# Decode attention with a gated FFN: one load for the first cache group, ring slots on 512-byte addresses, and two projections with the activations stationary

## The chip, the cores and the metric

The kernel runs on one core of one Trainium2 chip. The metric is device time in microseconds (us); less is better. Eight runs of the kernel before gave a median of 127.25 us, from 126.56 to 128.67.

## The reference, cut to what matters

Eight sequences decode one token each. The width D is 512; attention has 32 query heads and 8 key/value heads of 128, and looks at the last 1024 positions of a cache of 4096. All inputs are bf16.

```
xn = layernorm(x)                                   # x: 8 x 512
q  = xn @ wq                                        # wq: 512 x 4096
scores = einsum(q, k) * 128**-0.5                   # 4 query heads per key/value head
o  = softmax(scores) @ v                            # k, v: 8 x 8 x 1024 x 128 of the cache's window
s  = o.reshape(8, 4096) @ wo                        # wo: 4096 x 512
g  = silu((gelu(xn @ w_gate) * (xn @ w_up)) @ w_down)   # F = 1792
return x + s * g
```

The windows of k and v are 16 MiB each, wq and wo 4 MiB each, and the three FFN matrices 1.75 MiB each: 47.45 MB that are each read once.

## The kernel before, in words

The order of every engine's instructions is the order of the code (`manual_schedule`); there is no planner. All large loads are issued from SP into a ring of 22 SBUF slots of 8 KB per partition (`slot`, 1 MB each): first the keys of group 0, then the four row blocks of wq, then keys and values of the 16 groups in turn, then w_gate, w_up and w_down in two halves each, then wo in four blocks. A group is one key/value head and four sequences (I = 4): a slot holds its 4 x 1024 keys, 32 per partition. SP's loads use eight completion semaphores in rotation, which the four small loads of `xq_sb` on ACT's queue use as well. A load waits until the load that had its semaphore before has landed, so about eight are under way at once. From the 23rd slot on, a load waits also until PE has let go of the slot's old content.

Group 0 of the keys is loaded in four DMAs of 32 rows (L88, every fourth partition); all other groups in one DMA of 128 rows (L90).

PE works in blocks of eight key columns. `transpose_block` (L261) transposes eight 128x128 pieces of keys into PSUM, and DVE copies them to `kT` (L270). `score_block` (L272) multiplies them with the queries, and after four blocks ACT takes the exponentials (L288). `value_block` (L308) runs six blocks later: it sums the exponentials by a matmul with ones (L300) and multiplies them with the values (L313). Two key blocks are transposed before `project_q` (L242), which every score needs. `expand_out` and `select_out` (L333, L350) bring the attention output of eight heads into the layout in which wo is read.

`project_q` makes q already transposed: each 128x128 piece of wq is the stationary operand, and the eight columns of `xnT_sb` are streamed; 128 matmuls, then one DVE cast (L254). `ffn_up` (L377) does the same with w_gate and w_up: 2 x 14 x 4 = 112 matmuls, for which every seventh column of a half of F is picked as stationary. The chain of elementwise steps for gelu (L393 to L406) works on 128 x 112 values. `ffn_down` (L408) and `project_out` (L364) have the activations stationary (8 columns) and stream the weights, in four column groups: output quarter q goes to PSUM partitions 32q to 32q+7.

At the end the program calls `expand_out(3)`, `ffn_up`, `select_out(3)`, `ffn_down`, `project_out(0)` to `(3)`, then the product `tmp` (L457), the sum with the residual `xq_sb`, which is bf16 (L459), and four stores of 2 KB.

PSUM: `ps_m` has two buffers of one bank; q, the sums, the outputs, the FFN results and the transposes of the tail all take them in turn.

SBUF: the pools `consts` and `persist` lie in front of the ring. In the built program the first slot starts at byte 25056 of a partition, which is 97 x 256 + 224; slots are 8192 bytes apart, so that all start 224 bytes past a multiple of 256.

Of the kernel before, what the change touches and what calls it, by code (L numbers as in the profile page):

```python
# [7 lines left out]
ACT = mybir.ActivationFunctionType  # L8
ALU = mybir.AluOpType
AX = mybir.AxisListType  # L10
BF16 = mybir.dt.bfloat16
FP32 = mybir.dt.float32
# [3 lines left out]
def kernel(  # L16
# [13 lines left out]
    nc = tc.nc  # L30

    B, Sq, D = A_x.shape
    Hkv, Sk, Dh = A_k_cache.shape[1], A_k_cache.shape[2], A_k_cache.shape[3]
    Hq = A_wq.shape[1] // Dh
    rep = Hq // Hkv
    W = min(4096, max(256, Sk // 4))
    win0 = Sk - W
    F = B_w_gate.shape[1]
    P = nc.NUM_PARTITIONS
    NDC = D // P  # L40
# [4 lines left out]
    I = 4  # L45
    R = P // I
    C = W // R
# [4 lines left out]
    NB = C // CB  # L52
    SLOT = C * Dh

    JF = F // 2 // P
    NQ = D // P

    consts = ctx.enter_context(tc.tile_pool(name="consts", bufs=1))
    persist = ctx.enter_context(tc.tile_pool(name="persist", bufs=1))
    ring = ctx.enter_context(tc.tile_pool(name="ring", bufs=22))  # L60
    kT_pool = ctx.enter_context(tc.tile_pool(name="kT_pool", bufs=4))
    p_pool = ctx.enter_context(tc.tile_pool(name="p_pool", bufs=3))
    small = ctx.enter_context(tc.tile_pool(name="small", bufs=3))
# [2 lines left out]
    ps_m = ctx.enter_context(tc.tile_pool(name="ps_m", bufs=2, space=bass.MemoryType.PSUM))  # L66
# [9 lines left out]
    def slot():  # L76
        return ring.tile([P, SLOT], BF16, name="slot")

    k_t, v_t, wo_t = {}, {}, {}
    wq_t, wg_t, wu_t, wd_t = [], [], [], []  # L80

    def load_cache(src, g, split=False):
        t = slot()
        hkv, b0 = g // GPH, (g % GPH) * I
        rows = src[b0 : b0 + I, hkv, win0:Sk, :].rearrange("i (r c) d -> i r (c d)", c=C)
        if split:
            for i in range(I):
                nc.sync.dma_start(out=t[i::I, :], in_=rows[i])  # L88
        else:
            nc.sync.dma_start(out=t, in_=rows.rearrange("i r m -> r i m"))  # L90
        return t

    def load_k(g, split=False):
        k_t[g] = load_cache(A_k_cache, g, split)

    def load_v(g):
        v_t[g] = load_cache(A_v_cache, g)
# [7 lines left out]
    def load_ffn():  # L105
        for dst, src in ((wg_t, B_w_gate), (wu_t, B_w_up)):
            for a in range(2):
                t = slot()
                nc.sync.dma_start(
                    out=t[:, 0 : 2 * F],  # L110
                    in_=src[a * 2 * P : (a + 1) * 2 * P, :].rearrange(
                        "(p k) f -> p (k f)", k=2
                    ),
                )
                dst.append(t[:, 0 : 2 * F].rearrange("p (k f) -> p k f", k=2))
        for a in range(2):
            t = slot()
            nc.sync.dma_start(
                out=t[:, 0 : JF * D],
                in_=B_w_down[a * JF * P : (a + 1) * JF * P, :].rearrange(  # L120
                    "(p j) d -> p (j d)", j=JF
                ),
            )
            wd_t.append(t[:, 0 : JF * D].rearrange("p (j d) -> p j d", j=JF))


    HS = SLOT // D
# [8 lines left out]
                nc.sync.dma_start(out=t[:, lo:hi, :], in_=src[:, lo:hi, :])  # L136
        wo_t[m] = t

    load_k(0, split=True)
    load_wq()  # L140
    for g in range(1, NG):
        load_k(g)
# [3 lines left out]
    for m in range(NM):  # L146
# [3 lines left out]
    ident = consts.tile([P, P], BF16, name="ident")  # L150
    nc.vector.memset(ident, 0.0)
    nc.gpsimd.affine_select(  # L152
        out=ident, in_=ident, compare_op=ALU.not_equal, fill=1.0, base=0,
# [10 lines left out]
        out=sel, in_=sel, compare_op=ALU.not_equal, fill=1.0, base=0,  # L164
# [4 lines left out]
        out=diag, in_=sel.rearrange("p r i -> p i r"), axis=AX.X, op=ALU.add  # L169
    )  # L170
    nc.vector.tensor_scalar(
        out=diag, in0=diag, scalar1=1.0, scalar2=30000.0, op0=ALU.subtract, op1=ALU.mult
# [6 lines left out]
        out=hmask, in_=hmask, compare_op=ALU.is_ge, fill=0.0, base=0,  # L179
# [3 lines left out]
        out=hmask, in_=hmask, compare_op=ALU.is_ge, fill=0.0, base=B - 1,  # L183
# [5 lines left out]
        out=bsel3, in_=bsel3, compare_op=ALU.not_equal, fill=1.0, base=0,  # L189
# [4 lines left out]
        out=bsel_f, in_=bsel3.rearrange("p h b -> p b h"), axis=AX.X, op=ALU.add  # L194
# [5 lines left out]
    xq_sb = persist.tile([P, P], BF16, name="xq_sb")  # L200
# [17 lines left out]
        op0=ALU.subtract, op1=ALU.mult,  # L218
    )

    xnT_sb = persist.tile([P, NDC, B], BF16, name="xnT_sb")
    xpT_sb = persist.tile([P, NDC, B], BF16, name="xpT_sb")
    qT_all = persist.tile([P, Hkv, B, rep], BF16, name="qT_all")
    oT_all = persist.tile([P, Hq, B], BF16, name="oT_all")
    hT_sb = persist.tile([P, 2 * JF, B], BF16, name="hT_sb")
    g_sb = persist.tile([P, P], FP32, name="g_sb")

    s_ps = ps_s.tile([P, P], FP32, name="s_ps")
# [2 lines left out]
    def transpose_x():  # L231
        t = ps_m.tile([P, 2, NDC, B], BF16, name="m_ps")
        for k in range(NDC):
            nc.tensor.transpose(t[:, 0, k, :], xhat[:, k * P : (k + 1) * P], ident[0:B, 0:B])  # L234
        xp = xhat.rearrange("b (a p k) -> b a k p", a=2, k=2)
        for a in range(2):
            for k in range(2):
                nc.tensor.transpose(t[:, 1, 2 * a + k, :], xp[:, a, k, :], ident[0:B, 0:B])
        nc.vector.tensor_copy(out=xnT_sb, in_=t[:, 0])
        nc.vector.tensor_copy(out=xpT_sb, in_=t[:, 1])  # L240

    def project_q():  # L242
        q_ps = ps_m.tile([P, Hq, B], FP32, name="m_ps")
        for k in range(NDC):
            for h in range(Hq):
                nc.tensor.matmul(  # L246
                    q_ps[:, h, :],
                    wq_t[k][:, h * Dh : (h + 1) * Dh],
                    xnT_sb[:, k, :],
                    start=(k == 0 and h == 0),  # L250
                    stop=(k == NDC - 1),
                    skip_group_check=True,
                )
        nc.vector.tensor_copy(  # L254
            out=qT_all, in_=q_ps.rearrange("p (h j) b -> p h b j", j=rep)
        )


    kT, sc, pT, oT = {}, {}, {}, {}
# [114 lines left out]
                )  # L374


    def ffn_up():  # L377
        gu_ps = ps_m.tile([P, 2, 2 * JF, B], FP32, name="m_ps")
        for w, wt in enumerate((wg_t, wu_t)):
            for j in range(2 * JF):  # L380
                f0 = (j // JF) * (F // 2) + j % JF
                for k in range(NDC):
                    nc.tensor.matmul(  # L383
                        gu_ps[:, w, j, :],
                        wt[k // 2][:, k % 2, f0 : f0 + (P - 1) * JF + 1 : JF],
                        xpT_sb[:, k, :],
                        start=(k == 0),
                        stop=(k == NDC - 1),
                    )
        shape = [P, 2 * JF, B]  # L390
        zT, uT = gu_ps[:, 0], gu_ps[:, 1]
        z2 = persist.tile(shape, FP32, name="z2")
        nc.scalar.activation(out=z2, in_=zT, func=ACT.Square)  # L393
        nc.vector.tensor_scalar(  # L394
            out=z2, in0=z2, scalar1=0.044715, scalar2=1.0, op0=ALU.mult, op1=ALU.add
        )
        u3 = persist.tile(shape, FP32, name="u3")
        nc.vector.tensor_tensor(out=u3, in0=z2, in1=zT, op=ALU.mult)
        th = persist.tile(shape, FP32, name="th")
        nc.scalar.activation(out=th, in_=u3, func=ACT.Tanh, scale=0.7978845608028654)  # L400
        nc.vector.tensor_scalar(
            out=th, in0=th, scalar1=0.5, scalar2=0.5, op0=ALU.mult, op1=ALU.add
        )
        gz = persist.tile(shape, FP32, name="gz")
        nc.vector.tensor_tensor(out=gz, in0=th, in1=zT, op=ALU.mult)
        nc.vector.tensor_tensor(out=hT_sb, in0=gz, in1=uT, op=ALU.mult)  # L406

    def ffn_down():  # L408
        f_ps = ps_m.tile([P, P], FP32, name="m_ps")
        nc.vector.memset(f_ps, 0.0)  # L410
        for j in range(2 * JF):
            for q in range(NQ):
                nc.tensor.matmul(
                    f_ps[32 * q : 32 * q + B, :],
                    hT_sb[:, j, :],
                    wd_t[j // JF][:, j % JF, q * P : (q + 1) * P],
                    start=(j == 0),
                    stop=(j == 2 * JF - 1),
                    skip_group_check=True,
                )  # L420
        th2 = persist.tile([P, P], FP32, name="th2")
        nc.scalar.activation(out=th2, in_=f_ps, func=ACT.Tanh, scale=0.5)
        nc.vector.tensor_scalar(
            out=th2, in0=th2, scalar1=0.5, scalar2=0.5, op0=ALU.mult, op1=ALU.add
        )
        nc.vector.tensor_tensor(out=g_sb, in0=th2, in1=f_ps, op=ALU.mult)
# [8 lines left out]
    for n in range(N + LAG):  # L435
# [4 lines left out]
        if n >= LAG:  # L440
            g, s = (n - LAG) // NB, (n - LAG) % NB
# [8 lines left out]
    ffn_up()  # L450
    select_out(NM - 1)
    ffn_down()
    for m in range(NM):
        project_out(m)

    tmp = small.tile([P, P], FP32, name="tmp")
    nc.vector.tensor_tensor(out=tmp, in0=s_ps, in1=g_sb, op=ALU.mult)  # L457
    out_sb = small.tile([P, P], BF16, name="out_sb")
    nc.vector.tensor_tensor(out=out_sb, in0=tmp, in1=xq_sb, op=ALU.add)  # L459
    for q in range(NQ):  # L460
        eng = nc.sync if q % 2 == 0 else nc.scalar
        eng.dma_start(
# [32 lines left out]
```

## Time and profile before

| | |
|---|---|
| median of 8 runs | 127.25 us (126.56 to 128.67) |
| profiled execution, its own time | 127.12 us |
| its span in the profile | 125.4 us |
| PE, DVE, ACT busy | 66%, 54%, 17% of the span |
| read from HBM | 47.46 MB, 379 GB/s over the span |
| first load issued / first data | 0.80 us / about 2.0 us |
| last matmuls start / end of the last sum | 120.73 us / 122.49 us |

The span runs from the first instruction to the last; the execution's own time is 1.7 us more. The page of the profile shows busy time by engine, the span in 40 slices of 3.135 us with the rate of the DMA engines, the chain of work that ended last, groups of instructions by source line, and the DMA issues. The other views are answers of the trace: stretches of time with the busy time of each engine, waits, and the instructions in order of time. "Landing" is the time from a DMA's issue until it has arrived in full.

### The profile page before, as it was taken

Reading aid. Unit: us, or ns where it says so; the run is one execution under the profiler, and the core shown is the slowest. Engines: PE = TensorE matmul, PEld = TensorE weight load, DVE = VectorE, ACT = ScalarE, POOL = GpSimd, SP = SyncE. Lnnn points to the kernel's source line nnn. Section 1 sums busy time; section 2 is a strip of 40 time slices with the busy share of each in tenths; the row PEclk is TensorE's granted clock in tenths of the full one; section 3 lists DMA queues with packets and bytes.
Section 4 is the critical chain, followed back from the end, with each engine's and each line's share of the span. In section 5 each row is a group of like instructions: output and inputs, shape, how many; then the busy total and the mean of one; then the engine's idle time right before and its main releaser. Section 6 shows DMA issues by size and latency. Waiting matters only on the chain.

```text
span 125.4 us, 4445 instructions
## 1 busy us (share of the span) xinstructions
PE 82.4 (66%) x2020; PEld 76.6 (61%) x2020; DVE 68.2 (54%) x145; ACT 21.9 (17%) x70; POOL 2.1 (2%) x13
## 2 busy tenths in 40 slices
PE   0063359766967867878694993969798737836450
PEld 0062359765957857768583993859698637826340
DVE  2361005846858659786595983956999640041010
ACT  0540000303303213032030330303023300010000
POOL 6000000000000000000000000000000000000000
PEclk9999999999999999999999999976999955555555
DMA  3999999999999999999999999999999999999710
GB/s 99 292 330 413 426 421 421 421 415 421 413 421 418 413 418 405 423 418 418 410 421 410 421 418 421 421 408 421 413 423 402 421 414 412 420 416 416 278 54 5
DMA packets 6978, 47.75 MB, mean 381 GB/s; under 512 B 936, under 2 KB 944, under 8 KB 1968
## 3 DMA queue, kind: packets, MB, share of 16 engines
q1 hardware_dynamic: 6848, 47.46, 92.7%
q8 instruction: 15, 0.25, 0.8%
q10 hardware_dynamic: 112, 0.02, 0.1%
q14 instruction: 3, 0.02, 0.1%
HBM read 47.46 MB, written 0.01 MB: 379 GB/s over the span
## 4 chain that ended last, share of the span: by engine, by line
DMA 93%; POOL 1%; PE 1%; issue 1%; DVE 0%; POOLq 0%; ACTq 0%; SPq 0%; DVEq 0%
DMA slot<-in_A_k_cache_dram 60%; DMA slot<-in_B_w_gate_dram 16%; DMA slot<-in_A_wo_dram 14%; DMA xq_sb<-in_A_x_dram 3%; PE s_ps L367 1%; POOL sel L163 0%; POOLq L490 0%; DVE tmp L457 0%; POOL ident L152 0%; DVE out_sb L459 0%; ACTq L203 0%; POOL hmask L178 0%; POOL hmask L182 0%; POOL sel L162 0%; POOL xq_sb L201 0%
## 5 line engine op out<-in xcount | busy, mean ns | idle before, releaser
L270 DVE COPY kT<-kT_ps 128x1024 bf16<-128x1024 bf16 x64 | 41.9, 676 | 20.6 <-PE kT_ps L266 20.0
L266 PE MATMUL kT_ps<-ident,slot 128*128 128x128 bf16 x512 | 41.9, 229 | 14.2 <-DMA slot<-in_A_k_cache_dram 14.2
L266 PEld LDWEIGHTS <-slot 128*128 128x128 bf16 x512 | 31.4, 102 | 18.1 <-DMA slot<-in_A_k_cache_dram 15.2
L288 ACT ACTIVATE pT<-sc_ps,diag 128x128 bf16<-128x128 f32 x64 | 18.2, 368 | 73.2 <-PE sc_ps L278 73.2
L278 PE MATMUL sc_ps<-qT_all,kT 128*128 128x16 bf16 x512 | 22.5, 171 | 0.0
L313 PE MATMUL m_ps<-pT,slot 128*128 128x16 bf16 x512 | 21.7, 170 | 0.3 <-issue 0.3
L313 PEld LDWEIGHTS <-slot 128*128 128x128 bf16 x512 | 18.3, 96 | 3.2 <-issue 1.6
L278 PEld LDWEIGHTS <-kT 128*128 128x128 bf16 x512 | 19.9, 97 | 0.0
L302 DVE TENSOR_REDUCE sums<-m_ps 128x16 f32<-128x512 f32 x16 | 10.9, 682 | 1.0 <-PE m_ps L300 1.0
L383 PE MATMUL m_ps<-xpT_sb,slot 128*128 128x8 bf16 x112 | 6.5, 195 | 2.5 <-DMA slot<-in_B_w_gate_dram 1.4
L246 PE MATMUL m_ps<-xnT_sb,slot 128*128 128x8 bf16 x128 | 4.1, 168 | 5.9 <-DMA slot<-in_A_wq_dram 5.9
L383 PEld LDWEIGHTS <-slot 128*128 128x128 bf16 x112 | 6.2, 153 | 2.8 <-DMA slot<-in_B_w_gate_dram 1.5
L246 PEld LDWEIGHTS <-slot 128*128 128x128 bf16 x128 | 3.7, 104 | 6.4 <-DMA slot<-in_A_wq_dram 6.4
L300 PE MATMUL m_ps<-pT,ones_pp 128*128 128x512 bf16 x16 | 6.2, 387 | 0.7 <-ACT pT L288 0.7
L367 PE MATMUL s_ps<-slot,oE 128*8 128x128 bf16 x128 | 4.2, 307 | 3.6 <-DMA slot<-in_A_wo_dram 3.6
L367 PEld LDWEIGHTS <-oE 128*8 128x8 bf16 x128 | 3.4, 119 | 4.3 <-issue 4.2
L254 DVE CAST qT_all<-m_ps 128x256 bf16<-128x256 f32 x1 | 0.4, 426 | 9.3 <-PE m_ps L246 9.3
L340 DVE TENSOR_TENSOR wide<-m_ps,hmask 64x1024 bf16<-64x1024 bf16 x4 | 4.9, 1216 | 0.5 <-PE m_ps L336 0.4
L234 PE MATMUL m_ps<-ident,xhat 8*128 8x8 bf16 x4 | 0.3, 168 | 6.9 <-DVE xhat L216 6.9
L394 DVE TENSOR_SCALAR z<-z 128x112 f32<-128x112 f32 x1 | 0.2, 219 | 8.0 <-ACT z L393 8.0
L234 PEld LDWEIGHTS <-xhat 8*128 8x128 bf16 x4 | 0.2, 103 | 6.9 <-DVE xhat L216 6.9
L306 DVE RECIPROCAL recip<-sums 128x16 f32<-128x16 f32 x16 | 4.0, 253 | 0.6
(53 smaller groups left out, 25.0 us busy)
## 6 DMA issues: line engine op xcount, KB each, us to landing
slot<-in_A_v_cache_dram SPq DMA_DIRECT2D x16, 1024.0 KB, 19.9
slot<-in_A_k_cache_dram SPq DMA_DIRECT2D x15, 1024.0 KB, 20.6
slot<-in_A_wq_dram SPq DMA_DIRECT2D x4, 1024.0 KB, 9.5
slot<-in_A_wo_dram SPq DMA_DIRECT2D x3, 1024.0 KB, 18.7
slot<-in_B_w_gate_dram SPq DMA_DIRECT2D x2, 896.0 KB
slot<-in_B_w_up_dram SPq DMA_DIRECT2D x2, 896.0 KB
slot<-in_B_w_down_dram SPq DMA_DIRECT2D x2, 896.0 KB
slot<-in_A_k_cache_dram SPq DMA_DIRECT2D x4, 256.0 KB, 3.9
```

The costliest lines, as they stand in the source:

```text
L246: nc.tensor.matmul(q_ps[:, h, :], wq_t[k][:, h * Dh : (h + 1) * Dh], xnT_sb[:, k, :], start=(k == 0 and h == 0), stop=(k == NDC - 1), skip ...
L266: nc.tensor.transpose(t_ps[:, c * P : (c + 1) * P], k_t[g][:, cc * Dh : (cc + 1) * Dh], ident)
L270: nc.vector.tensor_copy(out=kT[n], in_=t_ps)
L278: nc.tensor.matmul(sc[g][:, s * CB + c, :], kT[n][:, c * P : (c + 1) * P], qT_all[:, hkv, b0 : b0 + I, :], start=True, stop=True,)
L288: nc.scalar.activation(out=pT[g][:, :, i * rep : (i + 1) * rep], in_=sc[g][:, :, i * rep : (i + 1) * rep], func=ACT.Exp, bias=diag[:, i : ...
L300: nc.tensor.matmul(sums_ps, ones_pp, pT[g], start=True, stop=True)
L302: nc.vector.tensor_reduce(out=sums, in_=sums_ps.rearrange("p c m -> p m c"), axis=AX.X, op=ALU.add)
L306: nc.vector.reciprocal(out=recip[g], in_=sums)
L313: nc.tensor.matmul(oT[g], v_t[g][:, c * Dh : (c + 1) * Dh], pT[g][:, c, :], start=(c == 0), stop=(c == C - 1),)
L340: nc.vector.tensor_tensor(out=wide, in0=t_ps.rearrange("p (q e) -> p e q", e=HS) .unsqueeze(2) .to_broadcast([HS * B, HS, HS, DQ]), in1=hm ...
L367: nc.tensor.matmul(s_ps[32 * q : 32 * q + B, :], oE[m][:, e, :], wo_t[m][:, e, q * P : (q + 1) * P], start=(m == 0 and e == 0), stop=(m == ...
L383: nc.tensor.matmul(gu_ps[:, w, j, :], wt[k // 2][:, k % 2, f0 : f0 + (P - 1) * JF + 1 : JF], xpT_sb[:, k, :], start=(k == 0), stop=(k == N ...
```

## The change

1. **First key group.** `load_cache` loses its split form. Group 0 is loaded like all others, in one DMA of 128 rows.
2. **Ring.** The pool `ring` is made ahead of `consts` and `persist`, behind a pad of 384 bytes. The first slot starts at byte 16896, which is 33 x 512, and so all slots start on multiples of 512. There are 21 instead of 22.
3. **q projection.** The activations are stationary (`xnT_sb` widened from 8 to 32 columns, the added ones zero), the weights are streamed 512 columns at a time, in four column groups; 32 matmuls fill two PSUM banks. Two DVE casts, eight PE transposes and two DVE copies then bring q into the layout `qT_all` that the scores use.
4. **FFN up.** Likewise: 32 matmuls of 512 columns. The streamed columns of the weights are picked with a step of 14 elements (28 bytes). The two results lie in two banks as 128 x 512; since 14 column blocks are dealt out to four groups of four, two are computed twice. The gelu chain works on 128 x 512 values. Four PE transposes and a DVE copy make `hT_sb`. w_down is loaded as "(p j) d" over all of F, in two halves of seven j.
5. **Residual.** `xq_sb` is copied to fp32 (`xr_sb`) after `ffn_down`, and the last sum reads the copy.

```diff
-    JF = F // 2 // P
+    JF = F // P
     NQ = D // P
+    JQ = 4
+    Q = 32
+    front = ctx.enter_context(tc.tile_pool(name="front", bufs=1))
+    front.tile([P, 96], FP32, name="front_pad")
+    ring = ctx.enter_context(tc.tile_pool(name="ring", bufs=21))
     consts = ctx.enter_context(tc.tile_pool(name="consts", bufs=1))
     persist = ctx.enter_context(tc.tile_pool(name="persist", bufs=1))
-    ring = ctx.enter_context(tc.tile_pool(name="ring", bufs=22))
...
-        rows = src[b0 : b0 + I, hkv, win0:Sk, :].rearrange("i (r c) d -> i r (c d)", c=C)
-        if split:
-            for i in range(I):
-                nc.sync.dma_start(out=t[i::I, :], in_=rows[i])
-        else:
-            nc.sync.dma_start(out=t, in_=rows.rearrange("i r m -> r i m"))
+        rows = src[b0 : b0 + I, hkv, win0:Sk, :].rearrange("i (r c) d -> r i (c d)", c=C)
+        nc.sync.dma_start(out=t, in_=rows)
         return t
...
+        JH = JF // 2
+        wd = B_w_down.rearrange("(p j) d -> p j d", j=JF)
         for a in range(2):
-            t = slot()
-            nc.sync.dma_start(
...
+            t = slot()[:, 0 : JH * D].rearrange("p (j d) -> p j d", j=JH)
+            nc.sync.dma_start(out=t, in_=wd[:, a * JH : (a + 1) * JH, :])
+            wd_t.extend(t[:, j, :] for j in range(JH))
...
-    load_k(0, split=True)
+    load_k(0)
...
+    xnT_sb = persist.tile([P, NDC, Q], BF16, name="xnT_sb")
+    xpT_sb = persist.tile([P, NDC, Q], BF16, name="xpT_sb")
+    nc.gpsimd.memset(xnT_sb, 0.0)
+    nc.gpsimd.memset(xpT_sb, 0.0)
...
     def project_q():
-        q_ps = ps_m.tile([P, Hq, B], FP32, name="m_ps")
+        NW = rep * Dh
+        q_sb = persist.tile([P, Hkv // NQ, NW], BF16, name="q_sb")
+        q_ps = [ps_m.tile([P, NW], FP32, name="m_ps") for n in range(Hkv // NQ)]
         for k in range(NDC):
-            for h in range(Hq):
+            for hkv in range(Hkv):
+                n, q = hkv // NQ, hkv % NQ
                 nc.tensor.matmul(
-                    q_ps[:, h, :],
-                    wq_t[k][:, h * Dh : (h + 1) * Dh],
+                    q_ps[n][Q * q : Q * (q + 1), :],
                     xnT_sb[:, k, :],
+                    wq_t[k][:, hkv * NW : (hkv + 1) * NW],
...
+        for n in range(Hkv // NQ):
+            nc.vector.tensor_copy(out=q_sb[:, n, :], in_=q_ps[n])
+        t_ps = ps_m.tile([P, Hkv // NQ, rep, NQ, Q], BF16, name="m_ps")
+        for n in range(Hkv // NQ):
+            for j in range(rep):
+                nc.tensor.transpose(
+                    t_ps[:, n, j].rearrange("p q r -> p (q r)"),
+                    q_sb[:, n, j * Dh : (j + 1) * Dh],
+                    ident,
+                )
+        for n in range(Hkv // NQ):
+            nc.vector.tensor_copy(
+                out=qT_all[:, n * NQ : (n + 1) * NQ],
+                in_=t_ps[:, n, :, :, 0:B].rearrange("p j q b -> p q b j"),
+            )
...
+    j0 = [min(q * JQ, JF - JQ) for q in range(NQ)]
     def ffn_up():
-        gu_ps = ps_m.tile([P, 2, 2 * JF, B], FP32, name="m_ps")
+        gu_ps = [ps_m.tile([P, JQ * P], FP32, name="m_ps") for w in range(2)]
         for w, wt in enumerate((wg_t, wu_t)):
-            for j in range(2 * JF):
-                f0 = (j // JF) * (F // 2) + j % JF
-                for k in range(NDC):
+            for k in range(NDC):
+                cols = wt[k // 2][:, k % 2, :].rearrange("x (p j) -> x j p", j=JF)
+                for q in range(NQ):
                     nc.tensor.matmul(
-                        gu_ps[:, w, j, :],
-                        wt[k // 2][:, k % 2, f0 : f0 + (P - 1) * JF + 1 : JF],
+                        gu_ps[w][Q * q : Q * (q + 1), :],
                         xpT_sb[:, k, :],
+                        cols[:, j0[q] : j0[q] + JQ, :],
...
+        h_sb = persist.tile(shape, BF16, name="h_sb")
+        nc.vector.tensor_tensor(out=h_sb, in0=z2, in1=uT, op=ALU.mult)
+        h_ps = ps_m.tile([P, JQ, P], BF16, name="m_ps")
+        for c in range(JQ):
+            nc.tensor.transpose(h_ps[:, c, :], h_sb[:, c * P : (c + 1) * P], ident)
+        nc.vector.tensor_copy(out=hT_sb, in_=h_ps)
...
+    xr_sb = persist.tile([P, P], FP32, name="xr_sb")
+    nc.vector.tensor_copy(out=xr_sb, in_=xq_sb)
     for m in range(NM):
         project_out(m)
...
-    nc.vector.tensor_tensor(out=out_sb, in0=tmp, in1=xq_sb, op=ALU.add)
+    nc.vector.tensor_tensor(out=out_sb, in0=tmp, in1=xr_sb, op=ALU.add)
```

## The prediction

> **What bounds the kernel now.** I read the slices of the span first, then the chain that ended last, then stretches of time, then the tail in order of time. The page:
>
> ```profile
> DMA  3999999999999999999999999999999999999710
> GB/s 99 292 330 413 426 421 421 421 415 421 413 421 418 413 418 405 423 418 418 410 421 410 421 418 421 421 408 421 413 423 402 421 414 412 420 416 416 278 54 5
> ...
> DMA 93%; POOL 1%; PE 1%; issue 1%; DVE 0%; POOLq 0%; ACTq 0%; SPq 0%; DVEq 0%
> ...
> slot<-in_A_k_cache_dram SPq DMA_DIRECT2D x4, 256.0 KB, 3.9
> ```
>
> The DMA engines are busy from the second slice to the 37th, and the chain is loads for 93% of the span; PE and DVE, 66% and 54% busy, follow. So the time is bytes over rate, plus what is lost at both ends. The three stretches (columns: busy us by engine, clock, DMA share, GB/s):
>
> ```profile
> 2.00:10.00 8.00, 2.19 (x24) 1.91 (x24) 4.14 (x13) 2.86 (x3) 1.06 (x7) 1.00 0.92 313
> 10.00:116.00 106.00, 77.12 (x1900) 72.28 (x1901) 63.25 (x127) 19.08 (x67) 0.00 (x0) 0.91 1.01 417
> 116.00:121.00 5.00, 2.32 (x76) 1.92 (x79) 0.00 (x0) 0.00 (x0) 0.00 (x0) 0.50 0.53 208
> ```
>
> The middle is steady at 417 GB/s. The first 8 us move (417 - 313) x 8 = 0.83 MB less than that rate would, worth 2.0 us. In the last 5 us some engines are done early; that is another loss, which no edit touches. SP's own waits up to 10 us:
>
> ```profile
> SPq L102 <- DMA slot<-in_A_k_cache_dram: 1.9, 3, 1.0
> SPq L90 <- DMA xq_sb<-in_A_x_dram: 0.6, 1, 0.6
> ```
>
> The four small loads hold four of the eight semaphores, so each wq load waits for one of them to land: all of wq is out only at 7.07 us, and until then there is little in the queues. The tail, in order of time:
>
> ```profile
> 116.36 1.02 PE L367 MATMUL s_ps<-slot,oE 128*8 128x128 bf16 x32 [1.31 <-DMA slot<-in_A_wo_dram]
> ...
> 120.73 1.03 PE L367 MATMUL s_ps<-slot,oE 128*8 128x128 bf16 x32 [0.86 <-DMA slot<-in_A_wo_dram]
> 121.82 0.29 DVE L457 TENSOR_TENSOR tmp<-s_ps,g_sb 128x128 f32<-128x128 f32 x1 [6.64 <-PE s_ps L367]
> 122.20 0.29 DVE L459 TENSOR_TENSOR out_sb<-tmp,xq_sb 128x128 bf16<-128x128 f32 x1
> ```
>
> The last wo block lands at 120.7; 1.8 us of work and the stores follow. PE waits for wo, not wo for PE.
>
> **What the skill says.** (1) "DMA: Bandwidth & Descriptors", How a descriptor splits into AXI transactions: a descriptor is cut into transactions of 256 B in beats of 32 B, and one that doesn't start on a multiple of 256 B pays beats for the bytes in front of its start. It doesn't say whether this holds where the start in SBUF is the odd one. The trace can't decide it: all ring rows before start 224 bytes off. (2) "SBUF — State Buffer", The DMA setup-cost knee: every transfer pays a fixed part, so one large one is better than several. The trace agrees: 256 KB took 3.9 us to land. (3) "TensorE: Matmul & The Clock Gate", Part 3: matmuls in different column groups run side by side. The trace agrees: the 32 matmuls of L367 take 1.03 us though one lasts 0.31, so they start (1.03 - 0.31) / 31 = 23 ns apart. (4) "SBUF — State Buffer", Door 1, the box on cachelines: reads that take a new 16-byte line for each element are slower. The 28-byte step of the new FFN operand is such a read; no run here shows its cost on a streamed operand.
>
> **The change part by part.**
>
> *One load for group 0.* SP issues one DMA (0.53 to 0.59 us in L90's rows) instead of four (2.48 us). It leaves the semaphores of three small loads free, so three wq loads follow at once, at 0.33 to 0.37 us each: 4 MB are queued by about 2.5 us, where before the last wq load went out at 6.5. The fourth wq load waits for group 0 to land; behind it k1, v0 and k2 wait for wq blocks 0 to 2; no engine needs these before q. At least 3 MB stay in flight, 7 us of work, so the engines don't run dry. The gain lies between 0 (the slow start is that of the memory and of the small packets of other queues) and the 2.0 us lost. From the start times in the trace's packet records, on average about 1.4 of the 16 engines have no packet between 2.3 and 9.5 us: 1.4/16 x 7.2 = 0.6 us, which the queued loads take back. The rest are packets of 0.4 to 1.1 us instead of 0.31; of these 1.4 us I give back a third. I take **1.0 us**.
>
> *Slots on 512.* An engine moves about 376 ring rows (6016 over 16), at 8192 x 16 / 417 GB/s = 314 ns for 8 KB. By the skill's account 224 bytes are 7 beats; a beat is 1.17 ns (8 KB rows take at least 309 ns and 2 KB rows 84 in the packet records: 225 ns for 192 beats). So at most 7 x 1.17 x 376 = 3.1 us; at least 0, if it is not the writing side that counts. The records bound it better: by that slope the ring's rows have a fixed part of 84 - 75 = 9 ns, the 1 KB rows of x, 32 bytes off, 44 - 37.5 = 6.5, and the 256 B stores, whose far end is aligned, 15 - 9.4 = 5.6. The difference is 2.5 to 3.4 ns; I take 3.5 ns: x 376 = **1.3 us**.
>
> *21 slots.* Only eight loads are under way, 20 us of stream; the ring is 21 slots of 2.5 us. A slot has to be let go 13 loads, 32 us, after it has landed; scores and values come one to two groups (5 to 10 us) after. 0.
>
> *q projection.* Before: 1.02 us of PE after wq's last block, 0.43 of cast. After: the last block's eight matmuls (two rounds of four side by side, 0.43 us a round at most), two casts of 512 columns at about 0.68 (the reduction of 128x512 in L302), eight transposes and the latency of one (about 0.8), two copies of half of L254's size (0.28 each): 0.9 + 1.4 + 0.8 + 0.6 = 3.7 us, 2.2 more. Behind it wait the first scores, then the ring. The loads go on meanwhile; between 20 and 40 us PE waits 4.4 us for keys and takes the delay up there. Without that cover it would be 2.2 us. 0 on the path. POOL's two added memsets (0.2 us each) come before 4 us; their reader runs at 7.3.
>
> *FFN up.* 112 matmuls become 32 of 512 columns. At half clock, as all of the tail is (0.50), with four side by side a round of four takes about 4 x 4 x 23 = 0.37 to 0.43 us: eight rounds, 3.4 us. They start as before at 101.1 and are paced by the halves of w_gate and w_up; a round needs only its half. w_up's last half lands at about 107, its two rounds end at 107.9. The gelu chain on 512 columns costs 0.7 us for each PSUM step and 0.3 to 0.6 for the others, about 3.3, but runs on w_gate's result during w_up. Then the last product (0.7), four transposes and a copy (0.9): `hT_sb` at 109.5, before 112.15. So `ffn_down` isn't late. How much slack: blocks 0 to 2 of `project_out` (1.0 each) must be done at 120.7, `ffn_down` (1.7) before them, hT's end (2.1) before that: w_up's matmuls may end at 113.8, 12.7 us after their start, 0.40 us a matmul. Even without side-by-side running, at 0.43, it would be 1 us late. 0 on the path.
>
> *Residual, w_down's order.* The fp32 copy (0.2 us) lies in DVE's 6.6 us wait for PE; the last sum is 128 columns either way (0.29; tmp with fp32 inputs 0.29). w_down's rows stay 7 KB runs. 322 fewer instructions make about one less of the 15 instruction fetches. 0.
>
> Sum: 127.12 - 1.0 - 1.3 = 124.8 for the profiled execution; the median of the runs shown is 0.13 higher: **124.9 us**. What is a gain to loads is a gain to the end, because nothing between the last landing and the end changes.
>
> **The rivals.**
>
> *R1, the FFN becomes the bound (slower).* If reads with a 28-byte step neither run side by side nor at full rate, a matmul could take 0.55 us: 32 x 0.55 = 17.6 instead of 12.7, 4.9 us late, against a stream 2.3 us earlier: 129.8. For it: the step takes a new line for every element, and four such streams at once. Against: PE's clock there is half, so a read has twice the time, and the weight loads of L383, with a 14-byte step, still pass at 56 matmuls in 3.15 us. It decides from 0.40 us a matmul; slower than before from 0.47.
>
> *R2, both gains full.* 7 beats a row and nearly all of the slow start: 3.1 + 1.5: 122.7.
>
> *R3, alignment is nothing.* The 417 are set elsewhere, as by memory; only the start gains 0.6 to 1.0: 126.3 to 126.6.
>
> *R4, nothing at all.* The slow start stays too, as the first packets of any queue are slow, and is only moved from keys to wq: 127.2.
>
> **How the numbers follow.** Forecast 50% (its own range 124.0 to 125.9), R2 17%, R3 13%, R4 10%, R1 10%. A difference under 0.5% (0.64 us) can't be told from no change here. Faster: forecast, R2 and most of R3, 78%; within: R4 and the rest of R3, 12%; slower: R1, 10%. From below, the range starts at R2's 122.7, so that a little of it falls out; above it ends at 126.9, which leaves R1 and half of R4 out.
>
> **What would show it.** Start: 2 to 10 us at over 360 GB/s, and wq's last block matmuls before 17 us (18.1 before). Alignment: the middle slices at 420 to 425 instead of 417; under 418 refutes it, 427 or more is R2. q: first score at about 19 to 20 us, and PE still waiting for keys before 40. FFN: its 32 matmuls end within 1.5 us of w_up's landing, and the chain at the end is a wo load followed by about 1 us of L383; R1 shows as a chain of PE through the FFN lines, with wo landed before. I would be wrong most likely through the fixed part of a row, for which the records give one indirect measure, or through the engines' uneven ends, which can swallow a gain in the rate.

## The result and the profile after

The changed kernel takes 123.19 us (median of 12 runs, 123.04 to 123.35). The kernel before, in the 35 runs set against it, takes 127.27 us (126.44 to 129.68). The ratio is 0.968, with a 95% interval from 0.966 to 0.971: 4.1 us or 3.2% faster, where 2.3 us had been forecast. The profiled execution took 123.24 us, its span is 121.2. The runs also lie closer together: 0.3 us from the lowest to the highest, against 3.2.

The page of the kernel after, with the slices (3.03 us each) and the chain that ended last:

```profile
span 121.2 us, 4123 instructions
...
DMA  3999999999999999999999999999999999999820
GB/s 87 411 411 427 427 425 425 419 422 433 422 433 425 414 414 422 430 422 433 425 430 417 427 422 425 414 427 422 433 427 418 424 417 420 428 433 419 342 83 5
...
DMA 95%; PE 1%; SPq 1%; DVE 0%; issue 0%
```

The rate is 411 GB/s or more from the second slice on, where it was 292 and 330 in the second and third slice before. The chain is still loads, now for 95%. The same three kinds of stretches of the kernel after (columns as before: busy us by engine, clock, DMA share, GB/s):

```profile
2.00:10.00 8.00, 3.06 (x32) 2.20 (x33) 4.15 (x13) 2.86 (x3) 1.34 (x9) 1.00 0.99 392
10.00:112.00 102.00, 80.74 (x1732) 67.45 (x1728) 67.49 (x132) 19.75 (x67) 0.00 (x0) 0.88 1.01 424
112.00:117.00 5.00, 1.89 (x76) 1.54 (x79) 0.00 (x0) 0.00 (x0) 0.00 (x0) 0.70 0.64 260
```

The last wo block lands at 116.72 us instead of 120.69, 4.0 us earlier. Where they come from: the first eight microseconds run at 392 instead of 313 GB/s, which is 0.63 MB, or 1.5 us at 424 GB/s. The middle runs at 424 instead of 417: the 44.2 MB that took 106.0 us take 104.2, 1.8 us. What is left, 0.7 us, lies in the last stretch: there the engines end less unevenly (260 GB/s before the last landing instead of 208, 0.26 MB more in 5 us). The runs don't tie this part to an edit: by the packet records the last 8 us before the last landing move less than the middle's rate would, and what is missing is worth 2.2 us before, 1.8 us after, and from 1.5 to 2.7 us in the other kernels of this study that start with four loads. The end of the kernel after, in order of time:

```profile
116.76 1.03 PE L383 MATMUL s_ps<-slot,oE 128*8 128x128 bf16 x32 [0.87 <-DMA slot<-in_A_wo_dram]
...
117.83 0.29 DVE L483 TENSOR_TENSOR tmp<-s_ps,g_sb 128x128 f32<-128x128 f32 x1 [7.48 <-PE s_ps L383]
118.16 0.29 DVE L485 TENSOR_TENSOR out_sb<-tmp,xr_sb 128x128 bf16<-128x128 f32 x1
```

It is what it was: PE waits for wo, one block of matmuls, two sums of 0.29 us. The fp32 residual changed nothing in the last sum.

### The profile page after: what moved, and what is told of

It is laid out like the page before. It is cut to its first block, busy times and chain, and to the rows that moved or that the text cites. A ratio compares the mean times of both kernels' runs of the same rounds, so it can differ in the third digit from the quotient of the medians.

```text
span 121.2 us, 4123 instructions
## 1 busy us (share of the span) xinstructions
PE 86.5 (71%) x1856; PEld 71.7 (59%) x1856; DVE 72.5 (60%) x150; ACT 22.6 (19%) x70; POOL 2.4 (2%) x15
## 4 chain that ended last, share of the span: by engine, by line
DMA 95%; PE 1%; SPq 1%; DVE 0%; issue 0%
DMA slot<-in_A_k_cache_dram 59%; DMA slot<-in_B_w_gate_dram 16%; DMA slot<-in_A_wo_dram 15%; DMA slot<-in_A_wq_dram 6%; PE s_ps L383 1%; SPq L91 1%; DVE tmp L483 0%; DVE out_sb L485 0%; SPq L134 0%; SPq L110 0%
## 5 line engine op out<-in xcount | busy, mean ns | idle before, releaser
L282 PE MATMUL kT_ps<-ident,slot 128*128 128x128 bf16 x512 | 45.1, 240 | 9.6 <-DMA slot<-in_A_k_cache_dram 9.1
L282 PEld LDWEIGHTS <-slot 128*128 128x128 bf16 x512 | 34.0, 107 | 13.3 <-DMA slot<-in_A_k_cache_dram 9.9
L294 PEld LDWEIGHTS <-kT 128*128 128x128 bf16 x512 | 20.8, 100 | 0.0
L329 PEld LDWEIGHTS <-slot 128*128 128x128 bf16 x512 | 18.5, 97 | 3.2 <-issue 1.7
L402 PE MATMUL m_ps<-slot,xpT_sb 128*32 128x512 bf16 x32 | 7.5, 1092 | 0.0
L383 PE MATMUL s_ps<-slot,oE 128*8 128x128 bf16 x128 | 3.3, 262 | 5.3 <-DMA slot<-in_A_wo_dram 5.3
L250 PE MATMUL m_ps<-slot,xnT_sb 128*32 128x512 bf16 x32 | 3.8, 560 | 4.0 <-DMA slot<-in_A_wq_dram 4.0
L383 PEld LDWEIGHTS <-oE 128*8 128x8 bf16 x128 | 2.6, 100 | 5.9 <-issue 5.9
L259 DVE CAST q_sb<-m_ps 128x512 bf16<-128x512 f32 x2 | 1.3, 686 | 6.6 <-PE m_ps L250 6.6
L250 PEld LDWEIGHTS <-xnT_sb 128*32 128x32 bf16 x32 | 0.9, 106 | 6.1 <-issue 5.8
L402 PEld LDWEIGHTS <-xpT_sb 128*32 128x32 bf16 x32 | 1.3, 112 | 4.4 <-issue 3.6
```

The costliest lines, as they stand in the source:

```text
L250: nc.tensor.matmul(q_ps[n][Q * q : Q * (q + 1), :], xnT_sb[:, k, :], wq_t[k][:, hkv * NW : (hkv + 1) * NW], start=(k == 0), stop=(k == NDC ...
L282: nc.tensor.transpose(t_ps[:, c * P : (c + 1) * P], k_t[g][:, cc * Dh : (cc + 1) * Dh], ident)
L294: nc.tensor.matmul(sc[g][:, s * CB + c, :], kT[n][:, c * P : (c + 1) * P], qT_all[:, hkv, b0 : b0 + I, :], start=True, stop=True,)
L329: nc.tensor.matmul(oT[g], v_t[g][:, c * Dh : (c + 1) * Dh], pT[g][:, c, :], start=(c == 0), stop=(c == C - 1),)
L383: nc.tensor.matmul(s_ps[32 * q : 32 * q + B, :], oE[m][:, e, :], wo_t[m][:, e, q * P : (q + 1) * P], start=(m == 0 and e == 0), stop=(m == ...
L402: nc.tensor.matmul(gu_ps[w][Q * q : Q * (q + 1), :], xpT_sb[:, k, :], cols[:, j0[q] : j0[q] + JQ, :], start=(k == 0), stop=(k == NDC - 1), ...
```

## The experiments

Twelve kernels were run, each against the kernel before on the same chip; there were four such sets of runs, each on a chip of its own. In all that follows "2 to 10" and "middle" are the DMA rates of the profiled execution from 2 to 10 us and from 10 to 112 us, and "row" is the mean time of an 8 KB row from 22 to 91.5 us, from the trace's packet records.

| kernel | us (lowest to highest, runs) | 2 to 10 | middle | row, ns |
|---|---|---|---|---|
| before | 127.27 (126.44 to 129.68, 35) | 313 | 417 | 316.3 |
| before, slots on 512 | 125.20 (124.86 to 125.38, 4) | 331 | 424 | 310.6 |
| before, one load for group 0 | 125.26 (125.03 to 125.49, 4) | 390 | 417 | 316.4 |
| before, both | 123.09 (123.07 to 123.25, 4) | 389 | 424 | 310.6 |
| after | 123.19 (123.04 to 123.35, 12) | 392 | 424 | 310.9 |

This table, whose kernels the following sections describe, is the result in short: each of the two load edits alone is worth about 2 us, the two together make up the whole gain, and the other edits give and cost nothing that these runs can tell.

The 2 us for one edit alone are a soft figure, because the kernel before spreads over 3 us, and its median was between 126.69 and 127.94 us in the four sets. Against the kernel before of its own set, the alignment gave 1.7 us (ratio 0.989, 95% interval 0.986 to 0.992) and the single load 1.4 us (0.988, 0.981 to 0.995). Between two kernels that both hardly spread, the alignment gave 2.2 us (125.26 to 123.09, on one chip).

### The offset of the slots

The packet records of the two kernels gave the first hint. With the slots on multiples of 512 nearly all 8 KB rows of the middle take 309 ns (3520 of 3565), and 7 KB rows 272; before, nearly all 8 KB rows lay between 309 and 324 ns, most of them at 313 or 320. The least times are the same in both kernels: 309 ns for 8 KB, 272 for 7 KB, 84 for 2 KB. So the fixed part of a row, on which the prediction's figure rested, hadn't changed. New theory: the offset makes rows scatter above their least time, by 5.4 ns on average, x 376 rows = 2.0 us. Three kernels move the slots within the changed kernel, and one aligns them in the kernel before.

*480 bytes past 512, as before:*

```diff
-    front.tile([P, 96], FP32, name="front_pad")
+    front.tile([P, 216], FP32, name="front_pad")
     ring = ctx.enter_context(tc.tile_pool(name="ring", bufs=21))
+    back = ctx.enter_context(tc.tile_pool(name="back", bufs=1))
+    back.tile([P, 8], FP32, name="back_pad")
```

> The kernel after, with the pad in front of the ring lengthened by 480 bytes, so that all slots lie 480 bytes past a multiple of 512, as in the kernel before (a second pad keeps everything behind the ring where it was within 512 bytes). Theory (the offset makes most 8 KB rows longer than 309 ns): the mean row goes from 312 to about 317 ns, the middle of the span from 424 back to 417 GB/s, time 125.2 us (376 rows x 5.4 ns = 2.0 more than 123.2). Rival (the rate rose because of something else, as fewer PE instructions or other PE traffic): rate 424 and time 123.2.

125.25 us (124.94 to 125.45), 2.06 more than the kernel after, and rows of 316.3 ns. The middle of this kernel:

```profile
10.00:112.00 102.00, 80.87 (x1700) 67.00 (x1696) 67.30 (x130) 19.75 (x67) 0.00 (x0) 0.90 1.01 417
```

The rate is 417 again, with PE's and DVE's work unchanged. Time, rate and row came out as the theory said.

*256 bytes past 512:*

```diff
-    front.tile([P, 96], FP32, name="front_pad")
+    front.tile([P, 160], FP32, name="front_pad")
     ring = ctx.enter_context(tc.tile_pool(name="ring", bufs=21))
+    back = ctx.enter_context(tc.tile_pool(name="back", bufs=1))
+    back.tile([P, 64], FP32, name="back_pad")
```

> The kernel after, with the slots 256 bytes past a multiple of 512. If what counts is 256-byte pieces, as the prediction reckoned, this is aligned: 123.2 us, 424 GB/s. If it is 512, it is like 480 bytes off: 125.2 us, 417 GB/s.

123.13 us (122.97 to 123.19), rows of 310.6 ns, and the middle:

```profile
10.00:112.00 102.00, 80.44 (x1732) 67.13 (x1728) 67.03 (x132) 19.75 (x67) 0.00 (x0) 0.92 1.01 424
```

Multiples of 256 bytes are enough. Against the run 480 bytes off, on the same chip, that is 2.1 us.

*128 bytes past 512* (a front pad of 128 and a back pad of 96 elements):

> The kernel after with the slots 128 bytes past a multiple of 512. Slots 256 bytes off were as fast as on 512, slots 480 bytes off 2 us slower. If pieces of 256 bytes count, 128 bytes off is slow: 125.2 us, 417 GB/s. If pieces of 128 or 64 bytes are enough: 123.2 us, 424 GB/s.

124.64 us (124.61 to 124.73), rows of 314.6 ns:

```profile
10.00:112.00 102.00, 81.96 (x1656) 67.69 (x1655) 67.15 (x129) 19.52 (x66) 0.00 (x0) 0.88 1.01 419
```

128 bytes off costs 1.45 us, 224 bytes past a multiple of 256 costs 2.06, 0 and 256 cost nothing. (The run 128 bytes off had no aligned kernel on its chip; 376 rows x 3.8 ns gives 1.4 us for it as well.) That fits the unit that the Trainium skill names ("DMA: Bandwidth & Descriptors", How a descriptor splits into AXI transactions: pieces of 256 B), now for starts in SBUF, of which the page doesn't speak. In size its account doesn't fit: at 32 B a beat, 128 and 224 bytes are 4 and 7 beats, which at the prediction's estimate of 1.17 ns a beat would be 4.7 and 8.2 ns a row; the rows were about 3.8 and 5.5 ns longer on average, and not by a constant. Why only some rows take the longer time isn't shown, nor is the mechanism.

*The kernel before with aligned slots alone:*

```diff
+    front = ctx.enter_context(tc.tile_pool(name="front", bufs=1))
+    front.tile([P, 8], FP32, name="front_pad")
     ring = ctx.enter_context(tc.tile_pool(name="ring", bufs=22))
+    back = ctx.enter_context(tc.tile_pool(name="back", bufs=1))
+    back.tile([P, 120], FP32, name="back_pad")
```

> The kernel before with nothing but a 32-byte pad in front of the ring (and one of 480 bytes behind it), so that its 22 slots lie on multiples of 512. Theory: middle of the span at 424 instead of 417 GB/s, time 127.25 - 2.0 = 125.3 us. Rival (alignment needs the other edits, or is nothing): 127.2.

125.20 us; on the same chip the kernel before took 126.9. Its middle:

```profile
10.00:112.00 102.00, 76.27 (x1880) 71.64 (x1884) 62.81 (x126) 18.85 (x67) 0.00 (x0) 0.92 1.01 424
```

A pad of 32 bytes does it. Over all fourteen profiles of this study the middle follows the offset and nothing else that was changed: 424 GB/s in the six kernels with slots on multiples of 256, 417 in the seven with slots 224 bytes past one, 419 at 128.

### The first load

*The changed kernel with four loads again* (`load_cache` with its split form, and `load_k(0, split=True)`):

> The kernel after, with group 0 loaded again in four DMAs of 32 rows. Theory (the four loads hold the semaphores for which the wq loads then wait, and the queues run thin): 2 to 10 us back at about 313 GB/s from 392, 0.63 MB or 1.5 us, time 124.7. Rival (the slow start belonged to the unaligned rows as well): 370 GB/s or more in 2 to 10 us, time 123.6 or less.

126.07 us in the median of nine runs from 124.95 to 127.46, above both expectations; the profiled one, the fastest, has 351 GB/s from 2 to 10 us, between the two. So four loads cost from 1.8 to 4.3 us here, and they bring back the spread of the runs. The median is 0.9 us above that of the kernel before with aligned slots (four runs on the same chip), which has four loads too; the lowest runs of the two (124.95 and 124.86) agree. Whether the other edits cost something behind a start with four loads isn't settled by this.

*The kernel before with one load:*

```diff
-    load_k(0, split=True)
+    load_k(0)
```

> The kernel before with group 0 in one load and nothing else. Theory: the start gains 1.5 to 1.75 us (2 to 10 us at 378 GB/s, as with slots 480 bytes off and one load), 125.3 us, and the runs draw together, since the four small loads are also what makes the runs of before spread over 3 us. Rival: the spread and the loss come from the rows of the ring; then 126 or more and a spread as before.

125.26 us, and only 0.5 us from lowest to highest; the kernel before took 126.69 on the same chip. Its first stretches:

```profile
2.00:10.00 8.00, 3.02 (x56) 2.92 (x56) 4.14 (x13) 2.86 (x3) 1.06 (x7) 1.00 0.98 390
10.00:112.00 102.00, 80.44 (x1816) 75.75 (x1820) 63.74 (x125) 18.94 (x66) 0.00 (x0) 0.83 1.01 417
```

The start is as in the kernel after, the middle as in the kernel before: the two edits act on different stretches.

*Both edits on the kernel before:*

> The kernel before with both load edits (slots on 512, one load for group 0), and with q, FFN up and the residual as before. Theory (PE's and DVE's edits are hidden under the loads): 123.2 us, within 0.4 of the kernel after. Rival (the new q or FFN gives or costs something): 0.6 us or more away from it; with the split form the kernel after was 0.9 us slower than the aligned kernel before, which would speak for a cost, so 122.4.

123.09 us (123.07 to 123.25), within 0.1 of the kernel after. The new q projection, the new FFN up, the fp32 residual and the one slot less give or cost no more than that.

Why are four loads slow? The prediction said that they hold the semaphores for which the wq loads wait. *The kernel before with the residual's four loads on POOL's queue*, where they hold none of the eight semaphores:

```diff
-        nc.scalar.dma_start(
+        nc.gpsimd.dma_start(
             out=xq_sb[32 * q : 32 * q + B, :], in_=x_flat[:, q * P : (q + 1) * P]
         )
```

> The kernel before, group 0 in four loads as ever, but the four small loads of the residual go out from POOL's queue, so that they hold none of the eight semaphores and three wq loads follow at once. Theory (the loss at the start is that the wq loads wait for semaphores): most of the 1.5 us comes back, 125.5 to 126.0 us. Rival (the loads of 32 rows are themselves slow): 126.9.

127.01 us (126.01 to 128.80, 12 runs), no gain: the kernel before took 126.69 on the same chip. SP's issues in this kernel, and two stretches:

```profile
0.81 2.47 SPq L88 DMA_DIRECT2D slot<-in_A_k_cache_dram  x4
3.32 2.27 SPq L102 DMA_DIRECT2D slot<-in_A_wq_dram  x4
```

```profile
5.00:6.00 1.00, 0.37 (x8) 0.29 (x8) 0.70 (x4) 1.00 (x1) 0.79 (x2) 1.00 0.64 205
6.00:10.00 4.00, 1.87 (x16) 1.63 (x16) 1.08 (x4) 0.04 (x1) 0.00 (x0) 1.00 0.99 356
```

The wq loads are out at 5.6 us instead of 7.1, without waiting, and still the DMA engines idle for a third of the time at 5 us. The waits for semaphores are not the cause, or not a cause by themselves. A second guess was the rows: a load of 32 rows writes every fourth partition only, and that might be what is slow. *Four loads that each cover 128 partitions with 2 KB of every row:*

```diff
-                nc.sync.dma_start(out=t[i::I, :], in_=rows[i])
+                m = C * Dh // I
+                nc.sync.dma_start(
+                    out=t[:, i * m : (i + 1) * m],
+                    in_=rows[:, :, i * m : (i + 1) * m].rearrange("i r m -> r i m"),
+                )
```

> The kernel before, group 0 still in four loads of 256 KB, but each covers all 128 partitions with 2 KB of every row instead of every fourth partition with 8 KB. Two wq loads are free of waits, two wait for parts of group 0. New theory (what is slow is the set of partitions that one load of 32 rows writes[...]; the semaphores and the number of loads are not it, since three free wq loads gave nothing): 2 to 10 us at 380 GB/s or more, 125.3 us as with one load. Rival (four small loads are slow because they are four): about 313 GB/s and 126.9 us.

127.73 us (126.96 to 129.46), 281 GB/s from 2 to 10 us, ratio to the kernel before 1.001 (0.998 to 1.004). That guess found no support either, though this form isn't clean: its rows are 2 KB, and two of the wq loads wait 4.1 us for parts of group 0. What both kernels and the kernel before share is that SP needs about 0.6 us to issue a load of 256 KB, which is about what the engines need to move it (256 KB at 424 GB/s is 0.62 us). The new theory is that no backlog forms, so that an engine that is done early has nothing to go on with. The last experiment changes the order alone: *the kernel with POOL's queue, and two wq loads ahead of the four:*

```diff
-    load_k(0, split=True)
-    load_wq()
+    load_wq((0, 1))
+    load_k(0, split=True)
+    load_wq((2, 3))
```

> The kernel before with its four loads of 32 rows for group 0, the small residual loads on POOL's queue as in the run of that name (127.0 us, 304 GB/s from 2 to 10 us), and two wq loads of 1 MB issued ahead of the four. Only the order of the loads differs from that run. Theory (four loads of 256 KB at the very start leave the engines without a backlog, SP needing about 0.6 us for each, whatever rows they write): behind 2 MB of backlog they cost nothing, 2 to 10 us at 380 GB/s or more, 125.3 to 125.5 us. Rival (loads of 256 KB are slow in themselves): 340 GB/s or less and 126.5 us or more.

125.20 us (125.14 to 125.44), where the same loads in the other order took 127.01. The two ran on different chips; against the kernel before of the own set the ratios are 0.983 (0.976 to 0.990) and 1.002 (0.998 to 1.006). SP's issues, and the first stretch:

```profile
0.81 0.89 SPq L102 DMA_DIRECT2D slot<-in_A_wq_dram  x2
1.75 3.26 SPq L88 DMA_DIRECT2D slot<-in_A_k_cache_dram  x4
```

```profile
2.00:10.00 8.00, 0.37 (x8) 0.29 (x8) 2.77 (x11) 2.29 (x3) 3.28 (x11) 1.00 0.95 383
```

The four loads of 32 rows cost nothing once 2 MB stand in front of them (one load for group 0 took 125.26), and the runs draw together as well (0.3 us instead of 2.8). So neither their number nor their rows cost anything in themselves: the loss is that of their place, a start without a backlog. It isn't only idleness. In the kernel before and in the run with POOL's queue, 8 KB rows of 0.4 to 1.1 us go on until about 9 us, also when all engines are busy again (6 to 10 us in the lines above: DMA share 0.99, 356 GB/s). In the kernel before with aligned slots they are nearly all over by 5 us, and 6 to 10 us runs at 423 GB/s. Why a thin start is followed by long rows, and for how long, stays open.

### The streamed operand with a step

In the changed kernel the FFN's matmuls are slower than reckoned:

```profile
98.60 7.55 PE L402 MATMUL m_ps<-slot,xpT_sb 128*32 128x512 bf16 x32
...
101.31 0.18 PEld L402 LDWEIGHTS <-xpT_sb 128*32 128x32 bf16 x4 [0.73 <-DMA slot<-in_B_w_up_dram]
102.23 0.18 PEld L402 LDWEIGHTS <-xpT_sb 128*32 128x32 bf16 x4 [0.73 <-issue]
```

From the weights of one round of four to the next it is 0.92 us (102.23 - 101.31), not 0.37 to 0.43. It is that at half clock (until about 100.4) and at full clock (from then on) alike; in the columns of stretches the clock is the third number from the end:

```profile
99.00:100.00 1.00, 1.00 (x8) 0.19 (x4) 0.92 (x1) 0.00 (x0) 0.00 (x0) 0.50 0.99 416
102.00:103.00 1.00, 1.00 (x8) 0.18 (x4) 0.00 (x0) 0.50 (x1) 0.00 (x0) 1.00 0.96 396
```

In each of the two microseconds eight matmuls are in work and the weights of four are loaded. *The same with 512 adjacent columns:*

```diff
-                        cols[:, j0[q] : j0[q] + JQ, :],
+                        wt[k // 2][:, k % 2, j0[q] * P : (j0[q] + JQ) * P],
```

> The kernel after, with FFN up streaming 512 adjacent columns instead of columns 28 bytes apart; the hidden columns are so permuted against w_down, which changes what is computed and nothing else. In the kernel after a round of four matmuls takes 0.91 us. Theory (the step of 28 bytes[...] is what makes it slow): a round of 0.22 to 0.43 us, the 32 matmuls paced by the loads; time the same, 123.2, as all this is hidden. Rival (512 columns in four groups are that slow anyway): 0.91 us a round.

```profile
98.52 1.96 PE L402 MATMUL m_ps<-slot,xpT_sb 128*32 128x512 bf16 x16
101.01 1.04 PE L402 MATMUL m_ps<-slot,xpT_sb 128*32 128x512 bf16 x8 [0.54 <-DMA slot<-in_B_w_up_dram]
103.14 1.04 PE L402 MATMUL m_ps<-slot,xpT_sb 128*32 128x512 bf16 x8 [1.08 <-DMA slot<-in_B_w_up_dram]
```

Now PE waits for w_up, and a round takes 0.43 us (99.35 - 98.92 between the weight loads of two rounds, at half clock). The time is 123.21 us, as after. So at half clock the 28-byte step costs 0.49 us a round. At full clock it costs more, as adjacent columns get faster with the clock. The matmuls of q have the same shape, and here are two rounds of them in the kernel after, at a clock of 1.00:

```profile
13.32 0.62 PE L250 MATMUL m_ps<-slot,xnT_sb 128*32 128x512 bf16 x8 [1.59 <-DMA slot<-in_A_wq_dram]
```

One matmul takes 0.39 us there, so that the second round starts 0.23 us after the first, where the stepped rounds of FFN up are 0.92 us apart. In the kernel after, two rounds of FFN up run at half clock and six at full, so the step costs some 5 us in all (an estimate: 2 x 0.49 + 6 x 0.69), and all of it is hidden: in the kernel after `hT_sb` is there at 107.9 us, and the first `project_out` still waits for its wo block at 110.0.

### The other edits alone

*The changed kernel with both load edits taken back:*

> The kernel after with both load edits taken back (group 0 in four loads, slots 480 bytes past 512): what is left are the new q projection, FFN up, the residual and one slot less. Theory (these are hidden): 126.9 us, as before, with a start at about 313 GB/s and a middle at 417. Rival (they cost something in this setting; with aligned slots and four loads the kernel after took 126.07, the kernel before 125.2): 127.7.

128.13 us (four runs from 127.37 to 129.81) against 127.94 for the kernel before in the same set; the ratio 1.010 has an interval from 0.996 to 1.025. That doesn't tell a cost from none, since starts with four loads spread, with the one exception of the aligned kernel before. The comparison without spread, 123.19 against 123.09 above, shows none above 0.1 us where the stream starts with one load; behind four loads it stays open.

## Why the prediction was right, and where its sizes were off

**What bounds the kernel** was right: the gain of the loads came out at the end (4.0 us at the last landing, 4.1 in the time), and the edits to PE and DVE gave and cost nothing.

**One load** was taken at 1.0 us between bounds of 0 and 2.0; alone it measured 1.4 us against the kernel before on its chip, 2.0 against all its runs. What was mis-sized is the share of the long rows: they went away for the most part, not by a third, and 2 to 10 us came to 390 GB/s, 1.5 us of stream. The rest lies in the uneven ends, which no edit was said to touch and which differ from kernel to kernel without a cause that the runs show. The reason given was also half wrong. The thin queue was right, as the run with two wq loads in front shows; that the semaphores made it thin was not, as the start stayed slow without them.

**Slots on 512** was the term of the sum that failed in its reasoning: 1.3 us from a difference in the fixed part of a row, between rows of other sizes on other queues. That fixed part is the same on and off the boundary (least times of 309, 272 and 84 ns in both kernels); what changes is how many rows take longer than the least time. The upper bound held (3.1 us; 2.06 measured), and the unit of 256 B too; only the inference between the bounds did not. The mean row, 316.3 to 310.9 ns, x 376, would have been the figure, and it can't be had from the kernel before. That the figure came within a factor of two of what was measured was luck, since it was read from something that doesn't change.

**21 slots** and the **residual** cost nothing, as said (123.09 against 123.19).

**q projection**: said to end later after wq's last block by 2.2 us, hidden, with first scores at about 19 to 20 us. The trace of the kernel after:

```profile
15.77 1.05 PE L250 MATMUL m_ps<-slot,xnT_sb 128*32 128x512 bf16 x8 [1.84 <-DMA slot<-in_A_wq_dram]
16.44 1.29 DVE L259 CAST q_sb<-m_ps 128x512 bf16<-128x512 f32 x2 [6.58 <-PE m_ps L250]
...
18.43 0.49 DVE L269 COPY qT_all<-m_ps 128x128 bf16<-128x128 bf16 x2 [0.70 <-PE m_ps L263]
...
19.04 0.41 PE L294 MATMUL sc_ps<-qT_all,kT 128*128 128x16 bf16 x8
```

From wq's last block (15.77) to the end of the copies (18.92) it is 3.15 us (3.7 reckoned; 1.48 before, from 18.08 to 19.56). Since wq's last block comes 2.3 us earlier, the first score starts at 19.0 instead of 19.8. PE still waits 4.2 us for keys between 20 and 40 us, so the cover was there.

**FFN up** was reckoned at 0.43 us a round and took 0.92. The sign that the prediction asked for, an end within 1.5 us of w_up's landing, failed: with adjacent columns the last rounds start at 103.1 us when w_up is there, while with the step the matmuls run until 106.15. The slack held: 0.236 us a matmul, against the 0.40 from which the rival R1 would have decided. So the price was wrong by a factor of two, and the forecast stood because the slack had been worked out with the price left open.

**The rivals.** R1 didn't happen, R3 and R4 fell with the two runs of single edits. The outcome, 123.19, lies below the forecast's own range (from 124.0) and nearer to R2 (122.7) than to the forecast (124.9). R2 was right on the start (1.5 us) and on both gains being large, but not on 7 full beats a row: 5.5 ns, not 8.2. Both gains of the forecast were too small, by 0.4 to 1.0 us and by 0.8, while its direction and the path that it named came out as reasoned.

## What to carry to other kernels

When loads set the end, look at the start addresses of their SBUF tiles: here rows of 8 KB that start on a multiple of 256 bytes moved 1.7% faster than rows 224 bytes off, and a pad of 32 bytes was all it took. Begin the stream with large loads: here four loads of 256 KB, each issued in the time that it takes to move, cost 1.4 to 2.9 us in the median and in most kernels made the runs spread, and the same four behind 2 MB cost nothing. An edit off the path needs no exact price if the slack is worked out, down to what one instruction may take.

## What the runs showed of the hardware that I hadn't expected

The time of an 8 KB row within a back-to-back stream: 310.6 to 310.9 ns on average at offsets 0 and 256, 314.6 at 128, 316.3 at 224 past a multiple of 256, with the same least time of 309 ns in all. A streamed matmul operand with a step of 28 bytes, in four column groups of 512 columns: 0.92 us a round at half and at full clock, against 0.43 at half clock and 0.23 at full clock for adjacent columns. A start without a backlog lowered the DMA rate until 5 us in one profile and until about 9 us in others, and in all such kernels but one the runs spread over 2.4 to 3.2 us, where they spread over 0.1 to 0.5 us in the kernels with a backlog.
